# Weight reloads of a recurrent attention layer: keys in rows of 3072 bytes instead of 1536, output weights in three transfers instead of six

## The chip, the cores and the metric

The kernel runs on one core of one Trainium2 chip. The metric is the device time of one execution in microseconds (us), lower is better. Each version is executed several times; one further execution is taken with the hardware profiler and gives the page and the trace that are read below.

## The reference, cut to what matters

Four layers alternate, A, B, A, B. Each is added to a residual stream `x` of 2048 rows and 640 columns in bf16. Layer A is the one that this change touches. It is recurrent: the 2048 rows are cut into 64 segments of 32 rows, each segment is attended together with 8 memory rows, and the memory of a segment is the output of the segment before.

```python
# layer A: 32 heads of 192; M = 8 memory rows, seg_len = 32
mem = mem0
for s in range(n_seg):                                # 64 segments, one after the other
    xs = x[:, s * seg_len:(s + 1) * seg_len, :].copy()
    h = jnp.concatenate([mem, xs], axis=1)            # 40 rows of 640
    q = jnp.einsum('btd,dhe->bhte', h, Wq)            # 640 -> 32 x 192
    k = jnp.einsum('btd,dhe->bhte', h, Wk)
    v = jnp.einsum('btd,dhe->bhte', h, Wv)
    scores = jnp.einsum('bhqe,bhke->bhqk', q, k) * scale
    scores = jnp.where(mask[None, None], scores, -1000000000.0)
    p = _softmax(scores, axis=-1)
    o = jnp.einsum('bhqk,bhke->bhqe', p, v)
    o = jnp.einsum('bhte,hed->btd', o, Wo)            # 32 x 192 -> 640
    mem = o[:, :M, :].copy()                          # feeds the next segment
    outs.append(o[:, M:, :])
```

Layer B is a linear attention over all rows. It is not touched.

## The kernel before, in words

Layer A has two parts. `A_pre` (line 676) computes, for all segments at once, what belongs to the last 8 rows of each segment and doesn't depend on the recurrence. `A_chain` (line 863) then walks the 64 segments in order; it is the recurrent part, and both layers A together walk 128 segments.

The heads are worked on in four rounds (`NR = 4`), each with a quarter of the columns of every weight. A weight piece of one round is named by its matrix (Q, K or V), its round `r` and its block `b` of the 640 inputs (five blocks of 128); it holds 128 partitions of 1536 bf16 values, 3072 bytes a partition. The weights of all four rounds don't fit in the on-chip memory. Most pieces are resident. Of each matrix three pieces live in slots (`SLOTS`, line 18), which hold round 0 or round 3 in turn. So does the output weight of one round, `wo_end`, which is 128 partitions of 7680 values, 15,360 bytes a partition, and holds round 0 or round 3. Its source is `wo_rows`, a copy of the output weights of these rounds that the kernel lays out once in the order of use.

The order of rounds alternates from segment to segment (`rounds`, line 880: 0 1 2 3, then 3 2 1 0), so that a segment starts with the round that the segment before ended with. A segment has to fetch one round: the slots after the first round have been multiplied, and `wo_end` after the first round's output product.

- `project` (line 940) multiplies the segment's 32 new columns with the five pieces of a matrix, four matmuls for each piece. In the first round of a segment (`n == 0`) it takes the slots first and calls `load_slot` (line 618) for each as soon as the four matmuls that read it are in the program. `load_slot` issues one transfer of 3072-byte rows for a Q or V piece, and two of 1536-byte rows for a K piece (line 621). The K product (its view of the weights at lines 952 and 953 takes 32 columns of both halves) needs both halves.
- `wo_round` (line 1039) multiplies one round's attention output with that round's output weights, in six steps of four matmuls (`j` = 0, 2, 4, 6, 8, 10). Step `j` reads the 1280 values from column 640 j of `wo_end` or `wo_mid`, that is one sixth, which is one transfer of `load_wo` (line 635) of 2560-byte rows.
- In the round `n == 2` the program multiplies the first round's output weights (line 1124) and then reloads `wo_end` with `load_wo(order[L])` (line 1125). The last `wo_round` of the segment (line 1173) reads it.

The order of instructions on each engine is written out by hand (`tc.manual_schedule()`, line 870); the framework puts in the waits between engines and transfers. All reloads are issued by SyncE, in the order Q, K, V, `wo_end`. GpSimd issues the small transfers of the chain (`kqb`, `Vp`, `otb`, `xr`, `attn`). After the last `wo_round`, lines 1179 to 1186 turn its result into the memory columns of the next segment's `hT`, for which the next segment's first matmul waits. A few matmuls into a scratch tile (`keep_busy`, lines 1172 and 1175) stand before and after that last product.

Of the kernel before, what the change touches and what calls it, by code (L numbers as in the profile page):

```python
# [115 lines left out]
class Kernel:  # L116
# [468 lines left out]
    def layer_A(self, xn_dram, at_dram, li, x_raw=None):  # L585
        nc, tc = self.nc, self.tc
        KC, NSEG = self.KC, self.NSEG
        dram = self.dram
        NR = 4
        PW = 1536  # L590
        self.kqb_d = dram.tile([NSEG, P, NR, 192], BF16, name=f"kqb{li}")
        self.vb_d = dram.tile([NSEG, NR, 2, 8, 896], BF16, name=f"vb{li}")
        self.otb_d = dram.tile([NSEG, P, 384], BF16, name=f"otb{li}")
        wview = self.wview
        wov = self.A_Wo.rearrange("h d m -> (h d) m").rearrange("(c p) m -> p c m", p=P)
        low = self.view(0, LATE)
        at = LATE
        res, slot = {}, {}
        for r in (3, 2):
            for m in "KQV":  # L600
                for b in range(KC - (SLOTS[m] if r == 3 else 0)):
                    res[m, r, b] = low[:, len(res) * PW:len(res) * PW + PW]
        assert len(res) * PW * 2 == LATE
        for m, r, b in [(m, 0, b) for m in "KQV" for b in range(KC - SLOTS[m])] + \
                [(m, None, b) for m in "KQV" for b in range(KC - SLOTS[m], KC)] + [(m, 1, b) for m in "KQV" for b in range(KC)]:
            v = self.view(at, 2 * PW)
            at += 2 * PW
            if r is None:
                slot[m, b] = v
            else:  # L610
                res[m, r, b] = v
        holds = {}
        wo_mid = self.view(at, 24 * 1280)
        wo_end = self.view(at + 24 * 1280, 12 * 1280)
        assert at + 36 * 1280 == ARENA
        unread = set(res)

        def load_slot(m, r, b, whole=False):
            if holds.get((m, b)) != r:
                holds[m, b] = r  # L620
                w = PW if whole or m in "QV" else PW // 2
                for h in range(0, PW, w):
                    nc.sync.dma_start(out=slot[m, b][:, h:h + w], in_=wview[m][:, b, PW * r + h:PW * r + h + w])

        def load_matrix(m, r):
            for b in range(KC):
                if (m, r, b) in unread:
                    unread.remove((m, r, b))
                    nc.sync.dma_start(out=res[m, r, b], in_=wview[m][:, b, PW * r:PW * r + PW])
                elif (m, r, b) not in res:  # L630
                    load_slot(m, r, b, True)

        early = {(0, 4), (0, 5), (2, 4), (2, 5), (1, 0), (1, 1), (1, 2), (1, 3)}

        def load_wo(r, into=None, part=range(6)):
            t = into if into is not None else wo_end[:, :] if r in (0, 3) else wo_mid[:, 7680 * (r - 1):7680 * r]
            for k in part:
                tk = t[:, 1280 * k:1280 * k + 1280]
                if r in (0, 3):
                    self.last_load = nc.sync.dma_start(out=tk, in_=self.wo_rows[r // 3, :, 1280 * k:1280 * k + 1280])  # L640
                else:
                    c0 = 12 * r + (3 * k if k < 4 else 1 + 6 * (k - 4))
                    step = 2 if k < 4 else 3
                    nc.sync.dma_start(out=tk.rearrange("p (c m) -> p c m", m=640),
                                      in_=wov[:, c0:c0 + step + 1:step, :])

        def piece(m, r, b):
            assert (m, r, b) in res or holds[m, b] == r
            return res[m, r, b] if (m, r, b) in res else slot[m, b]

        if li == 0:
            self.wo_rows = dram.tile([2, P, 7680], BF16, name="wo_rows")

        def lay_out_wo(i):
            rows = self.wo_rows[i].rearrange("p (c m) -> p c m", m=640)
            src = wov[:, 36 * i:36 * i + 12, :].rearrange("p (a t) m -> p a t m", t=3)
            for t, to in ((0, rows[:, 0:8:2, :]), (2, rows[:, 1:8:2, :]), (1, rows[:, 8:12, :])):
                nc.sync.dma_start(out=to, in_=src[:, :, t, :])

        def early_wo():  # L660
            for r in (2, 0, 1):
                load_wo(r, part=[k for k in range(6) if (r, k) in early])

        def late_wo(r, part=range(6)):
            load_wo(r, part=[k for k in part if (r, k) not in early])

        self.A_pre(xn_dram, li, load_matrix, piece, wo_mid, wo_end, lay_out_wo, early_wo, x_raw)
        self.A_chain(xn_dram, at_dram, li, load_slot, piece, load_wo, late_wo, wo_mid, wo_end, low)
        self.post_args = at_dram, wo_mid, wo_end, low

    def two_heads(self, ap):
# [188 lines left out]
        if x_raw is None:  # L860
            self.small.close()

    def A_chain(self, xn_dram, at_dram, li, load_slot, piece, load_wo, late_wo, wo_mid, wo_end, low):
        nc, tc, KC, NSEG = self.nc, self.tc, self.KC, self.NSEG
        scale = float(self.Dh) ** -0.5
        NR = 4
        with tc.tile_pool(name=f"A{li}_ch", reuse_waits="tile", bufs=1) as sp, \
# [12 lines left out]
            def rounds(s):  # L880
                return range(NR) if s % 2 == 0 else range(NR - 1, -1, -1)
# [54 lines left out]
            def place_v():  # L936
                nc.gpsimd.tensor_copy(out=Vs[64:96, :], in_=Vs[96:P, :])  # L937
                fetch_v()
# [64 lines left out]
            def sums(S, E):  # L1003
                one = self.ones_blk[0:96, :]
                nc.tensor.matmul(S[:, 0:320], lhsT=ap3(one, [list(one.ap[0]), [0, P]]), rhs=E[0:96, 0:320], start=True,  # L1005
                                 stop=True, skip_group_check=True)
# [32 lines left out]
            def wo_round(W, r, first, last, OT=OT):  # L1039
                m0 = 16 * (r % 2)  # L1040
                w = wo_end[:, :] if r in (0, 3) else wo_mid[:, 7680 * (r - 1):7680 * r]
                for j in range(0, 12, 2):
                    for g in range(4):
                        i = j + g // 2
                        G, c = (i // 4, i % 4) if i < 8 else (i % 4 // 2, 4 + i % 2)
                        wi = w[:, 640 * i:640 * i + 640].rearrange("p (h e c) -> p e h c", h=2, e=2)
                        nc.tensor.matmul(W[32 * g:32 * g + 32, 0:320], lhsT=OT[:, c, m0 + 32 * G:m0 + 32 * G + 32],  # L1047
                                         rhs=wi[:, g % 2], start=(first and j == 0), stop=(last and j == 10),
                                         tile_position=(0, 32 * g), skip_group_check=True)
# [35 lines left out]
            for s in range(NSEG):  # L1085
                order = rounds(s)
                L = NR - 1

                def q_or_k(m, n):
                    ps = pqp.tile([P, 512], F32, name="ps_qk", tag="qk")  # L1090
                    project(hT, ps, m, n, s)
                    return to_raw(ps, "raw" if n else "OT" if m == "Q" else "rc")
# [28 lines left out]
                for n in range(1, L):  # L1121
                    raw = q_or_k("Q", n + 1)
                    if n == 2:
                        wo_round(W, order[0], True, False)
                        load_wo(order[L])
                        if s == NSEG - 1:
                            load_wo(3, low[:, 0:7680])
                    sums(S, E)
                    O = attend(E)
                    if n == 2:  # L1130
                        place_v()
                    S1 = scores(order[n])
                    rc = reciprocals(S)
                    E = weigh(S1)
                    S = S1
                    to_rows(raw, "Q", order[n + 1])
                    next_kq(s, n)
                    if n == 1 and s + 1 < NSEG:
                        xr = load_rows(s + 1)
                    if n == L - 1:  # L1140
                        to_rows(q_or_k("K", n + 1), "K")
                        scale_out(O, rc)
                    else:
                        rawk = q_or_k("K", n + 1)
                        scale_out(O, rc)
                        to_rows(rawk, "K")
                    store_tail(s, order[n - 1])
                    pv = values(n, pop, "v")
                    v_rows(pv, 0, "s")
                    v_rows(pv, 1, "s")  # L1150
# [27 lines left out]
                if s + 1 < NSEG:  # L1178
                    wt = sp.tile([P, 2, KC, 32], F32, name="wt", tag="rc")
                    wv = W[:, 0:320].rearrange("p (h j b) -> p h b j", h=2, b=KC)  # L1180
                    for b0, b1 in ((2, 5), (0, 2)):
                        nc.vector.transpose(out=wt[:, :, b0:b1, :], in_=wv[:, :, b0:b1, :])  # L1182
                        for h in range(2):
                            a, b = slice(64 * h, 64 * h + 64), slice(64 - 64 * h, 128 - 64 * h)
# [74 lines left out]
```

## Time and profile before

| quantity | value |
|---|---|
| median of 3 runs | 3784.3 us (3781.2 to 3788.56) |
| the profiled execution's own time | 3791.75 us |
| its span, first to last instruction | 3790.0 us |
| granted TensorE clock | 0.98 |
| busy share PE / PEld / DVE / ACT / POOL | 91% / 57% / 58% / 53% / 52% |
| moved by DMA | 933.27 MB, 246 GB/s over the span |
| moved in the two chains of segments (219 to 1610 us and 2132 to 3520 us) | 281 and 280 GB/s, DMA share 0.84 in both |
| one segment (from one first reload of Q, 1001.12 us, to the next, 1022.84 us) | 21.72 us |

PE is the matrix unit, PEld its loading of stationary operands, DVE, ACT and POOL are VectorE, ScalarE and GpSimd, and SPq is SyncE, which here only issues transfers. The page gives, in this order, the busy time of each engine, the span in 40 slices, the DMA queues, the chain of work that ended last, the costliest groups of instructions and the DMA issues. A group's line ends with the idle time of its engine just before it and with what ended that idle time. "DMA share" is the packets' summed time over 16 DMA engines, so a value about 1 says that all 16 worked all the time; it can be a little over 1 because packets of different queues overlap on an engine.

### The profile page before, as it was taken

What the parts mean: (1) busy time and instruction counts of PE and PEld (TensorE: products, weight loads), DVE (VectorE), ACT (ScalarE), POOL (GpSimd) and SP (SyncE); (2) the same over time, 40 slices, a digit from 0 to 9 for tenths busy, and PEclk for the clock granted to TensorE, in tenths of its full rate; (3) what the DMA queues carried; (4) which work ended last, traced back from release to release, by engine and by line L of the source; (5) the groups of instructions that cost most, each with busy time, mean ns of one, the idle gap of its engine ahead of it and who ended that gap; (6) DMA issues with size and microseconds to landing.
All of it is one profiled execution on the core that took longest, in us unless ns stands there. A gap on an engine that the chain in (4) does not pass through costs nothing.

```text
span 3790.0 us, 147033 instructions
## 1 busy us (share of the span) xinstructions
PE 3446.3 (91%) x60058; PEld 2175.8 (57%) x60222; DVE 2180.9 (58%) x5940; ACT 1999.4 (53%) x4517; POOL 1955.7 (52%) x4871
## 2 busy tenths in 40 slices
PE   9979999999999999889899899999999999998898
PEld 6745555555555555555377555555555555555553
DVE  5446656666666666446633566566566665665465
ACT  2345555555555555546423455555555555555463
POOL 3446656666666666430433466566566665664300
PEclk9999999999999999989899999999999999999999
DMA  8988888888888888820477888888888888888300
GB/s 300 308 277 275 290 268 281 288 267 290 283 272 287 274 283 286 294 89 1 143 253 216 276 282 288 267 287 279 268 287 277 278 282 273 272 284 292 104 1 28
DMA packets 531678, 933.27 MB, mean 246 GB/s; under 512 B 145458, under 2 KB 295690, under 8 KB 531002
## 3 DMA queue, kind: packets, MB, share of 16 engines
q1 hardware_dynamic: 428858, 818.87, 63.7%
q0 software_dynamic: 68480, 91.75, 7.9%
q10 hardware_dynamic: 33664, 13.24, 1.4%
q8 instruction: 472, 7.73, 0.9%
q14 instruction: 204, 1.67, 0.1%
HBM read 853.72 MB, written 73.40 MB: 245 GB/s over the span
## 4 chain that ended last, share of the span: by engine, by line
PE 27%; DMA 16%; issue 5%; DVE 4%; ACT 3%; POOL 2%; PEld 2%; SPq 0%; POOLq 0%; DVEq 0%; ACTq 0%
DMA arena<-wo_rows 12%; PE ps_qk L954 9%; PE ps_v L954 3%; DMA arena<-in_A_Wv_dram 2%; PE ps_w L1047 2%; PE ps_qk L391 2%; PE ps_s L994 2%; PE ps_pre L825 1%; PEld L825 1%; DVE wt L1182 1%; PE ps_v L421 1%; DVE hT L1185 1%; PE kv L431 1%; PE ps_o L1019 1%; ACT arena L89 1%
## 5 line engine op out<-in xcount | busy, mean ns | idle before, releaser
L954 PEld LDWEIGHTS <-hT 128*32 128x32 bf16 x30720 | 786.7, 96 | 654.0 <-issue 148.7
L954 PE MATMUL ps_qk<-arena,hT 128*32 128x384 bf16 x20480 | 982.6, 328 | 61.5 <-DVE hT L1185 31.0
L964 ACT ACTIVATE raw<-ps_qk 128x384 bf16<-128x384 f32 x896 | 439.9, 491 | 371.6 <-DVE QT L975 139.8
L954 PE MATMUL ps_v<-arena,hT 128*32 128x384 bf16 x10240 | 515.6, 327 | 79.3 <-DMA arena<-in_A_Wv_dram 74.8
L1047 PE MATMUL ps_w<-arena,OT 128*32 128x320 bf16 x9216 | 428.1, 304 | 83.2 <-DMA arena<-wo_rows 75.7
L981 ACT ACTIVATE Vp<-ps_v 64x384 bf16<-64x384 f32 x896 | 434.0, 484 | 73.2 <-PE ps_v L954 42.6
L973 DVE STREAM_TRANSPOSE QT<-raw 128x256 bf16<-128x256 bf16 x384 | 171.0, 445 | 476.2 <-PE ps_s L994 450.9
L969 DVE STREAM_TRANSPOSE KT<-raw 128x384 bf16<-128x384 bf16 x512 | 296.0, 578 | 174.4 <-ACT raw L964 166.3
L917 POOL DMA_DIRECT2D kqb<-kqb x512 | 288.3, 563 | 177.9 <-POOL KT L926 143.5
L1047 PEld LDWEIGHTS <-OT 128*32 128x32 bf16 x9216 | 231.6, 97 | 249.6 <-issue 111.7
L1037 POOL DMA_DIRECT2D otb<-otb x512 | 280.3, 547 | 167.4 <-POOL otb L1036 143.0
L906 ACT ACTIVATE half<-ps_w 64x160 f32<-64x160 f32 x256 | 76.5, 299 | 514.2 <-PE ps_qk L954 487.2
L1010 ACT ACTIVATE ps_s<-ps_s 128x320 f32<-128x320 f32 x512 | 217.3, 424 | 191.5 <-PE ps_s L1005 190.2
L937 POOL COPY Vp<-Vp 32x896 bf16<-32x896 bf16 x256 | 237.2, 926 | 70.6 <-PE ps_o L1019 52.4
L994 PE MATMUL ps_s<-QT,KT 128*96 128x80 bf16 (+1 forms) x3072 | 245.1, 217 | 24.2 <-POOL KT L926 7.0
L994 PEld LDWEIGHTS <-KT 128*96 128x96 bf16 x3072 | 221.3, 125 | 55.1 <-issue 40.9
L1031 DVE TENSOR_TENSOR OT<-ps_o,rc 64x160 bf16<-64x160 f32 x768 | 243.0, 316 | 9.8
L1019 PE MATMUL ps_o<-E,Vp 96*128 96x80 bf16 x4096 | 233.9, 202 | 1.0 <-ACT ps_s L1010 0.8
L1011 ACT ACTIVATE rc<-ps_s 128x320 f32<-128x320 f32 x512 | 224.1, 438 | 18.4 <-DVE OT L1031 1.6
L1027 DVE TENSOR_TENSOR OT<-ps_o,rc 128x320 bf16<-128x320 f32 x384 | 188.6, 491 | 74.4 <-ACT rc L1011 58.6
L1019 PEld LDWEIGHTS <-Vp 96*128 96x128 bf16 x4096 | 210.0, 100 | 32.0 <-ACT Vp L981 13.6
L1000 ACT ACTIVATE E<-ps_s 96x320 bf16<-96x320 f32 x512 | 218.1, 426 | 12.3 <-PE ps_s L994 9.0
(161 smaller groups left out, 5567.1 us busy)
## 6 DMA issues: line engine op xcount, KB each, us to landing
arena<-wo_rows SPq DMA_DIRECT2D x792, 320.0 KB, 6.7
arena<-in_A_Wq_dram SPq DMA_DIRECT2D x427, 384.0 KB, 4.4
arena<-in_A_Wv_dram SPq DMA_DIRECT2D x427, 384.0 KB, 6.9
arena<-in_A_Wk_dram SPq DMA_DIRECT2D x768, 192.0 KB, 6.3
kqb<-kqb POOLq DMA_DIRECT2D x512, 48.0 KB, 5.3
arena<-in_A_Wk_dram SPq DMA_DIRECT2D x43, 384.0 KB, 6.8
vb<-arena POOLq DMA_DIRECT2D x128, 112.0 KB, 6.0
Vp<-vb POOLq DMA_DIRECT2D x256, 56.0 KB, 5.7
```

Of the source, the lines that this page charges most:

```text
L917: nc.gpsimd.dma_start(out=kqb[:], in_=self.kqb_d[s, :, r, :])
L937: nc.gpsimd.tensor_copy(out=Vs[64:96, :], in_=Vs[96:P, :])
L954: nc.tensor.matmul(ps[32 * g:32 * g + 32, 0:384], lhsT=hT[:, b, :], rhs=rhs, start=(i == 0), stop=(i == KC - 1), tile_position=(0, 32 * g) ...
L964: nc.scalar.activation(out=raw, in_=ps[:, 0:384], func=ACT.Copy)
L969: nc.vector.transpose(out=KT[:, :, 0:64], in_=raw.rearrange("p (c j) -> p c j", j=64))
L981: nc.scalar.activation(out=o, in_=i, func=ACT.Copy)
L994: nc.tensor.matmul(S[0:96, c0:c0 + 80 * (q1 - q0)], lhsT=KT[:, 3 * x + i, :], rhs=QT[:, x, q0:q1, :], start=False, stop=(x == 1 and i == 2 ...
L1011: nc.scalar.activation(out=rc[:, :], in_=S[:, 0:320], func=ACT.Exp, scale=-1.0)
L1019: nc.tensor.matmul(O[:, 80 * c:80 * c + 80], lhsT=Vs[0:96, 448 * x + k:448 * x + k + 128], rhs=E[0:96, 160 * x + 80 * e:160 * x + 80 * e + ...
L1031: nc.vector.tensor_tensor(out=OT[h, 4:6, :], in0=ov[h, 4:6, :], in1=rv[h, :, e, :], op=ALU.mult)
L1037: nc.gpsimd.dma_start(out=self.otb_d[s, :, 96 * r:96 * r + 96], in_=ob[:, :])
L1047: nc.tensor.matmul(W[32 * g:32 * g + 32, 0:320], lhsT=OT[:, c, m0 + 32 * G:m0 + 32 * G + 32], rhs=wi[:, g % 2], start=(first and j == 0), ...
```

## The change

The keys' slots are filled by one transfer of 3072-byte rows each, like those of Q and V. The reload of `wo_end` inside the chain goes by a new function with three transfers of 5120-byte rows, each of which serves two steps of `wo_round`. The bytes, their addresses and the arithmetic stay the same, and so do the loads ahead of the chain (they filled K slots with whole rows already, and use `load_wo`).

```diff
-        def load_slot(m, r, b, whole=False):
+        def load_slot(m, r, b):
             if holds.get((m, b)) != r:
                 holds[m, b] = r
-                w = PW if whole or m in "QV" else PW // 2
-                for h in range(0, PW, w):
-                    nc.sync.dma_start(out=slot[m, b][:, h:h + w], in_=wview[m][:, b, PW * r + h:PW * r + h + w])
+                nc.sync.dma_start(out=slot[m, b], in_=wview[m][:, b, PW * r:PW * r + PW])
...
-                    load_slot(m, r, b, True)
+                    load_slot(m, r, b)
...
+        def reload_wo(r):
+            for c0 in (0, 2560, 5120):
+                nc.sync.dma_start(out=wo_end[:, c0:c0 + 2560], in_=self.wo_rows[r // 3, :, c0:c0 + 2560])
...
                     if n == 2:
                         wo_round(W, order[0], True, False)
-                        load_wo(order[L])
+                        reload_wo(order[L])
                         if s == NSEG - 1:
                             load_wo(3, low[:, 0:7680])
```

The rest of the diff hands `reload_wo` from `layer_A` to `A_chain`.

More of the change, by code (lines that the diff above doesn't have):

```diff
@@ L667, in layer_A @@
         self.A_pre(xn_dram, li, load_matrix, piece, wo_mid, wo_end, lay_out_wo, early_wo, x_raw)
-        self.A_chain(xn_dram, at_dram, li, load_slot, piece, load_wo, late_wo, wo_mid, wo_end, low)
+        self.A_chain(xn_dram, at_dram, li, load_slot, piece, load_wo, reload_wo, late_wo, wo_mid, wo_end, low)
         self.post_args = at_dram, wo_mid, wo_end, low
@@ L861, in A_pre, with A_chain @@
             self.small.close()
-    def A_chain(self, xn_dram, at_dram, li, load_slot, piece, load_wo, late_wo, wo_mid, wo_end, low):
+    def A_chain(self, xn_dram, at_dram, li, load_slot, piece, load_wo, reload_wo, late_wo, wo_mid, wo_end, low):
         nc, tc, KC, NSEG = self.nc, self.tc, self.KC, self.NSEG
```

## The prediction

> **What bounds the kernel now.** I began with the page. PE is busy 91% of the span, yet the chain that ended last gives PE only 27% and one transfer, the reload of `wo_end`, more than any line of PE:
>
> ```profile
> PE 3446.3 (91%) x60058; PEld 2175.8 (57%) x60222; DVE 2180.9 (58%) x5940; ACT 1999.4 (53%) x4517; POOL 1955.7 (52%) x4871
> ...
> PE 27%; DMA 16%; issue 5%; DVE 4%; ACT 3%; POOL 2%; PEld 2%; SPq 0%; POOLq 0%; DVEq 0%; ACTq 0%
> ```
>
> The waits of PE, longest in total first (us in total, times, longest), say where transfers stop it:
>
> ```profile
> PE ps_w L1047 <- DMA arena<-wo_rows: 75.7, 157, 0.9
> PE ps_v L954 <- DMA arena<-in_A_Wv_dram: 74.8, 108, 2.6
> PE ps_qk L954 <- DVE hT L1185: 31.0, 128, 0.4
> ```
>
> Over 128 segments that is 0.59 us a segment for output weights and 0.58 for V, the third row being the recurrence itself. The timeline of one segment (start, duration, instructions, in brackets the idle time before) shows both in place:
>
> ```profile
> 1001.12 1.28 SPq L623 DMA_DIRECT2D arena<-in_A_Wq_dram  x3
> 1002.52 2.92 SPq L623 DMA_DIRECT2D arena<-in_A_Wk_dram  x6
> 1005.66 2.13 SPq L623 DMA_DIRECT2D arena<-in_A_Wv_dram  x3
> 1010.76 2.71 SPq L640 DMA_DIRECT2D arena<-wo_rows  x6
> ...
> 1015.15 0.35 PE L954 MATMUL ps_v<-arena,hT 128*32 128x384 bf16 x4 [0.38 <-DMA arena<-in_A_Wv_dram]
> ...
> 1019.21 0.73 PE L1047 MATMUL ps_w<-arena,OT 128*32 128x320 bf16 x16
> 1020.42 0.32 PE L1047 MATMUL ps_w<-arena,OT 128*32 128x320 bf16 x4 [0.49 <-DMA arena<-wo_rows]
> 1021.24 0.32 PE L1047 MATMUL ps_w<-arena,OT 128*32 128x320 bf16 x4 [0.49 <-DMA arena<-wo_rows]
> ```
>
> Steps j = 8 and j = 10 of the last output product each wait for their own sixth. The memory of the next segment, and so its first reload, hangs on j = 10. That closes the loop: recurrence, release of slots, one queue of reloads, last sixth, recurrence. Is that queue full? Columns of the windows: us, busy PE, PEld, DVE, ACT, POOL, clock, DMA share, GB/s:
>
> ```profile
> 1014.00:1018.00 4.00, 3.62 (x77) 2.46 (x73) 3.38 (x9) 2.91 (x8) 1.74 (x7) 1.00 1.04 372
> 1018.00:1020.00 2.00, 1.92 (x48) 1.06 (x41) 1.24 (x4) 0.54 (x2) 1.64 (x6) 1.00 0.54 191
> 1020.00:1022.00 2.00, 1.08 (x24) 0.58 (x23) 0.38 (x1) 0.00 (x0) 1.07 (x3) 1.00 0.13 34
> ```
>
> Yes, until about 1018; then a few late DMA engines finish alone, and PE waits for the latest. So the time of a segment follows the work of the latest DMA engine on its share of the reloads.
>
> **What the Trainium skill says.** "DMA: Bandwidth & Descriptors", section "Why a DMA increments its semaphore by 16 and not by 1": a transfer counts as landed only when every engine it uses has finished. The windows agree: share 0.54, then 0.13, while PE still waits. Section "Why small descriptors are slow (HBM only)" states a fixed cost of about 3 cycles for each packet and finds joining rows worth it only at 256 bytes or less; the rows below show a cost that 1536-byte rows still feel. Section "SWDGE vs HWDGE vs iDMA" prefers packets of at most 4096 bytes, for GpSimd's transfers; this queue shows no row over 3072 bytes before the change, so 5120 is untested here.
>
> **What a row costs.** I looked for windows in which SyncE's queue carries one kind of row alone (packets, MB, share of 16 engines). K, V and output weights, from the DMA view of 1006.1 to 1009.0, 1010.9 to 1012.5 and 1014.2 to 1017.5:
>
> ```profile
> q1 hardware_dynamic: 684, 0.94, 93.8%
> ```
>
> ```profile
> q1 hardware_dynamic: 200, 0.56, 95.7%
> ```
>
> ```profile
> q1 hardware_dynamic: 517, 1.18, 96.2%
> ```
>
> Share x 16 x window length gives engine time: 43.5, 24.5 and 50.8 us. With two more segments each (K 44.6 us for 0.96 MB and 45.3 for 0.96; V 22.5 for 0.53 and 21.7 for 0.51; output weights 50.2 for 1.12 and 51.3 for 1.12) the sums are 133.4/2.86 = 46.7 ns a kilobyte (1000 bytes) for 1536-byte rows, 68.7/1.60 = 42.9 for 3072 and 152.3/3.42 = 44.5 for 2560. A row of 1536 costs 71.7 ns and one of 3072 costs 131.8, so the line is 11.6 ns a row and 39.1 ns a kilobyte. It gives 43.7 for 2560, near the 44.5 seen, and 41.4 for 5120 (an estimate outside the rows seen).
>
> **The change part by part**, for one segment.
>
> 1. Keys as whole rows: 3 pieces x 393,216 bytes / 16 engines = 73.7 kB an engine; 46.7 - 42.9 = 3.8 ns a kilobyte less: 0.28 us less engine time. The completions saved are in these figures.
> 2. Output weights: 1,966,080 / 16 = 122.9 kB an engine; 43.7 - 41.4 = 2.3 ns less: 0.28 us less. Bounds: nothing, if 5120-byte rows are cut and cost as now; 44.5 - 41.4 = 3.1 ns, that is 0.38 us. I take the line, as it fits three row lengths. Below zero is rival C.
> 3. Together 0.56 us. Packets of two queues overlap (share 1.04 to 1.07), so wall time of an engine falls by 0.56/1.05 = 0.53 us. The late engine has the same number of rows as the others and works back to back, so all of it should arrive at the end.
> 4. Coarser last transfer: j = 8 no longer runs ahead of the last sixth; after the landing come j = 8 and j = 10. A whole product of 24 matmuls takes 1.00 us, four take 0.32, so a step in flow is (1.00 - 0.32)/5 = 0.14 us. Cost 0.14 on the path. At most both lone steps follow each other, 0.32. The wait for the middle third costs nothing while the last third ends later.
> 5. Coarser first reload: its issue waits one step more of the first product, 0.14 us. SyncE has only the two other thirds and the next segment's Q behind it. The backlog of V hides it: V releases PE at 1015.15, over 4 us after the issue at 1010.76. Without that cover, 0.14 us.
> 6. Issues: 12 instead of 18 a segment. Six K issues take 2.92 us; V's follow about 1.4 us sooner. Worth nothing by itself, since the queue has work until then; it also removes SyncE's waits for earlier landings (127.3 us on Q's over the run). GpSimd's small transfers may wait behind a longer packet, some 0.1 us each; they are issued microseconds ahead.
> 7. V's landing moves 0.27 us earlier with part 1 (0.28/1.05), so PE reaches the last product sooner and the last third stays the later of the two.
>
> Sum: -0.53 + 0.14 = -0.39 us a segment. The first segment of each chain has other loads, so 126 segments: -49 us. The profiled execution of 3791.75 us (span 3790.0, 1.75 around it) becomes 3743; the same 49 us off the median of 3784.3 gives 3735.
>
> PE's wait of 1.17 us a segment caps what can be gained: 150 us over all.
>
> **The rivals.**
>
> A, the sum: 3735. For it speaks the back-to-back queue; against it, that 5120 bytes was extrapolated.
>
> B, the longer output rows bring nothing, because they are cut into packets of the old cost: 0.27 - 0.14 = 0.13 us, 16 us in all, 3768. The 4096-byte preference speaks for it, the straight line over three lengths against.
>
> C, slower: the queue moves bytes at a ceiling, so that a row's shorter time turns into waiting elsewhere, and the coarser last third remains: 0.14 x 126 = +18, 3802. It decides as soon as the engine time saved falls below 0.14/0.53 = 26% of the forecast. For it: at share 1.04 the core already moves 372 GB/s. Against it: windows with longer rows moved more (K 362, V 369, output weights 388 GB/s).
>
> D, the late engines are late through other traffic that stretches as the reloads shrink: half of the 0.53 arrives, -0.13 us, 3768 again.
>
> **How the numbers follow.** A 0.58, B 0.20, D 0.09, C 0.13. Case A reaches from the larger row saving without the coarser last step (0.66 x 126 = 83, so 3701) to half its sum (3760). The range goes down to 3700 and up past B and D to 3783, leaving out C and the tails. A measurement of this kernel can't tell under 0.2% (7.6 us) from no change. Faster by more: nearly all of A, most of B and D, 0.80; same 0.07; slower 0.13.
>
> **What would show it.** Right: SyncE's queue with about 110,600 packets fewer (768 transfers of 144, 128 rows and 16 completions each), half of them the keys'; its K windows near 43 ns a kilobyte and output windows near 41; PE's waits on `wo_rows` and V falling by a third or more together; two steps of the last product in flow after one wait; a segment near 21.3 us. Wrong: output windows at 44.5 or two packets to a row (B); equal GB/s with more time a packet (C); a longer tail after 1018 (D). If PE now waits for something that isn't a reload, my reading of the loop was wrong.

## The result, and the profile after

The changed kernel took 3788.13 us, the median of 12 runs (3773.48 to 3796.77), beside 3785.45 us for the kernel before in 12 runs (3775.25 to 3790.82). The ratio is 1.0003, with an interval from 0.9987 to 1.0018: no change that can be told, where 49 us less had been forecast. The profiled execution had a span of 3791.9 us, 3793.59 with what lies around it.

The change did what it says. The page of the changed kernel gives SyncE's queue (packets, MB, share of 16 engines):

```profile
q1 hardware_dynamic: 318266, 818.83, 62.0%
```

Before, the page had 428,858 packets and 63.7% there: 110,592 packets fewer for the same bytes, as worked out. In time of one DMA engine it is 0.637 x 3790.0 = 2414 us before and 0.620 x 3791.9 = 2351 us after, 63 us less, or 0.49 us for each of 128 segments. The forecast had 0.56. So the engines did save nearly what they were to save, and the time did not move. The rows of 5120 bytes stayed whole, so the cutting that rival B rested on didn't happen; in 1015 to 1018.2 us, where they are alone on the queue, the DMA view gives

```profile
q1 hardware_dynamic: 261, 1.18, 96.5%
```

that is 0.965 x 16 x 3.2 us / 1.18 MB = 41.9 ns a kilobyte, beside 43.0 in the window of the prediction before; three such windows together give 42.0, where the line had said 41.4 and the windows before had shown 44.5.

The end of a segment also looks as foretold. The timeline of PE shows one wait and then both last steps in flow, eight matmuls in 0.46 us:

```profile
1019.79 0.73 PE L1049 MATMUL ps_w<-arena,OT 128*32 128x320 bf16 x16
1021.30 0.46 PE L1049 MATMUL ps_w<-arena,OT 128*32 128x320 bf16 x8 [0.78 <-DMA arena<-wo_rows]
1021.57 0.84 PE L1057 MATMUL ps_idle<-arena,ident 128*32 128x384 bf16 x16
```

What PE waits for (us in total, times, longest) holds the surprise:

```profile
PE ps_w L1049 <- DMA arena<-wo_rows: 77.9, 105, 1.3
PE ps_v L956 <- DMA arena<-in_A_Wv_dram: 57.6, 88, 2.8
...
PE ps_v L956 <- issue: 10.9, 22, 1.2
PE ps_w L1049 <- issue: 10.0, 12, 1.9
...
PE ps_qk L956 <- issue: 8.0, 10, 1.4
```

The waits for output weights did not fall and V's fell by 17 us: together 135.5 us after 150.5, where the prediction had named a fall by a third as the sign of being right. And waits put down to "issue" grew, in which nothing that the profile names was missing; "issue waits" below means PE's. With a fourth row of 0.2 us they add up to 29.1 us. Before, the same sum was 6.1:

```profile
PE ps_qk L954 <- issue: 2.4, 5, 0.6
PE ps_v L954 <- issue: 2.2, 6, 0.6
PE ps_w L1047 <- issue: 1.5, 3, 1.1
```

What PE lacks there can be seen around one of them. PE had done 14 of the 24 matmuls of the segment's last product, had stopped in the middle of a step, where no wait for weights begins, and resumed at 608.00 us after 1.90 us:

```profile
608.00 0.58 PE L1049 MATMUL ps_w<-arena,OT 128*32 128x320 bf16 x10 [1.90 <-issue]
```

The DMA queues of 600 to 605.5 us and then of 605.5 to 607 us:

```profile
q1 hardware_dynamic: 381, 1.70, 80.5%
q0 software_dynamic: 130, 0.16, 8.5%
```

```profile
q0 software_dynamic: 37, 0.03, 6.9%
q8 instruction: 1, 0.02, 4.8%
q1 hardware_dynamic: 4, 0.02, 2.7%
```

By the packet records an instruction packet started at 597.57 us, while the reloads filled the queue, and the next one at 605.62 us, when SyncE's queue had nearly run dry; that one ended at 606.78, and PE went on 1.2 us after it. When it was asked for, the trace does not show, so this example doesn't show either that it stood behind the reloads. Nor is all of the 1.90 us its doing: the last third of the output weights landed at 606.65, 0.55 us after PE had stopped.

Such a packet has 16,384 bytes and takes 1.09 us, and there are 472 in either run, beside 120,280 matmuls and weight loads of PE. Each of the 26 issue waits over 0.5 us ended 1.2 to 1.6 us after the end of an instruction packet; for moments taken at random in the chains the median distance is 3.6 us. I conclude that PE had run out of instructions; the profile doesn't name it.

### The profile page after: what moved, and what is told of

It reads as the page before. It is cut to its first block, busy times and chain, and to the rows that moved or that the text cites. A ratio compares the mean times of both kernels' runs of the same rounds, so it can differ in the third digit from the quotient of the medians.

```text
span 3791.9 us, 145879 instructions
## 1 busy us (share of the span) xinstructions
PE 3436.2 (91%) x60058; PEld 2179.4 (57%) x60222; DVE 2181.4 (58%) x5940; ACT 1996.0 (53%) x4517; POOL 1955.4 (52%) x4871
## 4 chain that ended last, share of the span: by engine, by line
PE 44%; DMA 31%; issue 8%; DVE 6%; POOL 4%; ACT 3%; PEld 3%; SPq 0%; POOLq 0%; ACTq 0%; DVEq 0%
DMA arena<-wo_rows 23%; PE ps_qk L956 17%; PE ps_v L956 6%; PE ps_w L1049 5%; PE ps_s L996 3%; DVE wt L1184 2%; PEld L827 2%; DMA otb<-otb 2%; DMA arena<-in_A_Wv_dram 2%; DVE hT L1187 2%; PE ps_o L1021 2%; PE ps_s L1007 2%; PE ps_qk L391 2%; PE ps_s L991 1%; PE ps_pre L827 1%
## 5 line engine op out<-in xcount | busy, mean ns | idle before, releaser
L956 PE MATMUL ps_v<-arena,hT 128*32 128x384 bf16 x10240 | 515.7, 327 | 70.5 <-DMA arena<-in_A_Wv_dram 57.6
L1049 PE MATMUL ps_w<-arena,OT 128*32 128x320 bf16 x9216 | 417.2, 303 | 94.7 <-DMA arena<-wo_rows 77.9
```

The source lines that it names most:

```text
L956: nc.tensor.matmul(ps[32 * g:32 * g + 32, 0:384], lhsT=hT[:, b, :], rhs=rhs, start=(i == 0), stop=(i == KC - 1), tile_position=(0, 32 * g) ...
```

## The experiments

Ratios are to the kernel before, run beside each version on the same chip; 0.001 is 3.8 us. From the packet records I also worked out, over some 120 segments of each kernel, when the last reload packet of a segment ends after its first Q reload, and how long after that step 10 of the last product (`j` = 10) starts:

| kernel | last packet, us (standard error about 0.05) | step 10 after it, median us |
|---|---|---|
| before | 19.61 | 0.53 |
| changed | 19.39 | 0.66 |
| keys alone | 19.49 | 0.53 |
| output weights alone | 19.32 | 0.65 |
| thirds with short rows | 19.51 | 0.66 |

The last column closes the loop as the prediction read it: in most segments step 10 follows the last packet at the same distance, and the coarser last third adds 0.13 us (forecast 0.14). In the second column the changed kernel gains 0.22 us (standard error of a difference about 0.07) where the engines' mean saved 0.49. So less than half of the saving had reached the last packet.

Three theories stood at first. 1: the saved row time reaches the last packet only in part, and the coarse end eats most of that. 2: the forecast's terms are right, and some new wait cancels them. 3: the queue moves bytes at a ceiling (rival C).

### One part at a time

Keys alone (`e1_keys`, edit in the kernel before):

```diff
-                w = PW if whole or m in "QV" else PW // 2
+                w = PW
```

> The kernel before with only the keys changed: one transfer of 3072-byte rows to a K slot, output weights still in six. Theory 1 (the saved row time reaches the last landing only in part, and most of what does is eaten by the coarser last third): in the trace of the changed kernel V lands 0.09 us earlier in the segment, so -0.09 x 126 = -11 us, ratio 0.997, and two separate waits on output weights as before. Theory 2 (the forecast's terms are right, and a new wait that belongs to the whole change cancels them): -0.27 x 126 = -34 us, ratio 0.991. Theory 3 (the queue moves bytes at a ceiling): 0 us.

Measured: 1.0016 (1.0004 to 1.0027), 6 us slower, just clear of no change. SyncE's queue took 63.2% of 3781.2 us, 24 us less engine time, 0.19 us a segment where 0.28 had been forecast. The issue waits added up to 24.4 us. All three theories were off: a part that saves engine time makes the kernel a little slower, and the issue waits come with it.

Output weights alone (`e2_thirds`): `reload_wo` as in the change, `load_slot` as before.

> The kernel before with only the output weights changed: three transfers of 5120-byte rows, keys still in halves. Theory 1: the last landing gains 0.12 us and the coarser last third costs 0.18 to 0.20, so +0.06 to +0.08 us a segment, +8 to +10 us, ratio 1.002 to 1.003. Theory 2: -0.27 + 0.14 = -0.13 us, -16 us, ratio 0.996. Theory 3: +0.14 x 126 = +18 us or more, ratio 1.005.

Measured: 0.9976 (0.9968 to 0.9984), 9 us faster. The queue took 62.8% of 3778.2 us, 41 us less, 0.32 a segment (forecast 0.28). Issue waits 6.2 us, as before. Theory 3 falls, and the sign of theory 1 was wrong; this part comes near the prediction's number (-16 us). The mechanism does so less: 41 us of engine time less 16 for the coarse end would have made 25.

Thirds with rows that stay short (`e4_thirds_short`): gaps of 128 bytes in `wo_rows` keep the two rows of a transfer apart.

```diff
-            self.wo_rows = dram.tile([2, P, 7680], BF16, name="wo_rows")
+            self.wo_rows = dram.tile([2, P, 6 * 1344], BF16, name="wo_rows")
...
+            for c in (0, 2, 4):
+                nc.sync.dma_start(out=wo_end[:, 1280 * c:1280 * c + 2560].rearrange("p (k e) -> p k e", e=1280),
+                                  in_=self.wo_rows[r // 3].rearrange("p (k e) -> p k e", e=1344)[:, c:c + 2, 0:1280])
```

> The kernel before with three transfers for the output weights whose rows stay 2560 bytes (the copy in device memory is laid out with gaps of 128 bytes, so that the rows can't join), keys in halves. It has the coarser last third without the longer rows. Theory 1: +0.18 us a segment less 0.03 for fewer completions, +19 us, ratio 1.005. Theory 2: 0.14 - 0.03, +14 us, ratio 1.004. If the time is that of the kernel before, the coarser last third costs nothing and the cancelling wait is elsewhere.

Measured: 1.0022 (1.0013 to 1.0030), 8 us slower: the coarse end alone, less what fewer completions save. Against `e2_thirds` it prices the longer output rows by themselves: 0.9976 - 1.0022, 17 us, 0.14 us a segment. The engines' mean saved 31 us between these two (63.4% of 3792.3 and 62.8% of 3778.2). So about half of a saving in row time arrives (13 to 22 of 31 us, by the two intervals).

The last third in two transfers again (`e3_last_sixths`, edit in the changed kernel):

```diff
-            for c0 in (0, 2560, 5120):
-                nc.sync.dma_start(out=wo_end[:, c0:c0 + 2560], in_=self.wo_rows[r // 3, :, c0:c0 + 2560])
+            for c0, c1 in ((0, 2560), (2560, 5120), (5120, 6400), (6400, 7680)):
+                nc.sync.dma_start(out=wo_end[:, c0:c1], in_=self.wo_rows[r // 3, :, c0:c1])
```

> The changed kernel with the last third of the output weights in two transfers of 2560-byte rows again, so that step 8 of the last product can run ahead of step 10. Theory 1: the gains stay (0.09 for keys, about 0.10 for output weights) and the cost of the coarse end goes, so -0.19 us a segment, -24 us, ratio 0.994. Theory 2: -0.50 us, -63 us, ratio 0.983, unless the unknown wait is elsewhere, then 0. Theory 3: 0 us.

Measured: 0.9984 (0.9974 to 0.9994), 6 us faster than before and 7 faster than the changed kernel, the latter at the edge of what the two intervals can tell; 24 had been expected. Issue waits 26.1 us: whole keys, and they are there again.

### Is it the row length of keys, or how far SyncE runs ahead?

After these four runs: issue waits of 24 to 29 us with one transfer to a key piece, 6 to 10 with two. Two readings, both guesses so far. R: instruction packets wait longer between longer rows. D (not the prediction's rival D): SyncE runs further ahead, and they wait behind a deeper queue. In the built programs each transfer of SyncE waits on one of eight counters in turn, so on the landing of the eighth before it; in the kernel before this was a visible wait,

```profile
SPq L623 <- DMA arena<-in_A_Wq_dram: 127.3, 179, 2.6
```

which in the changed kernel is down to 9.4 us in 11 waits. With six transfers ahead of V instead of nine, V's first reload goes out at 3.1 us after the first Q reload instead of 5.0.

Whole rows in two transfers of 64 partitions (`e5_keys_by_partitions`):

```diff
-                w = PW if whole or m in "QV" else PW // 2
-                for h in range(0, PW, w):
-                    nc.sync.dma_start(out=slot[m, b][:, h:h + w], in_=wview[m][:, b, PW * r + h:PW * r + h + w])
+                n = P if whole or m in "QV" else P // 2
+                for p in range(0, P, n):
+                    nc.sync.dma_start(out=slot[m, b][p:p + n, :], in_=wview[m][p:p + n, b, PW * r:PW * r + PW])
```

> The kernel before with keys in whole rows of 3072 bytes, but still two transfers to a piece, each for 64 of the 128 partitions: the longer rows without the fewer transfers. In the three kernels with one transfer to a key piece PE's idle time put down to issue was 24 to 29 us over the run, in the three with two transfers 6 to 10, and each such wait over 0.5 us ended 1.2 to 1.6 us after an instruction fetch had landed. Theory D (depth: with fewer transfers SyncE runs further ahead, and PE's instruction fetches come late behind the deeper queue): issue waits back near 6 us, the row saving is left, about 0.10 us a segment: -13 us, ratio 0.9965. Theory R (row length: an instruction packet waits longer between long rows): issue waits 24 us as with whole rows, ratio 1.0016.

Measured: 1.0795 (1.0773 to 1.0817), at a granted clock of 0.964. The issue waits added up to 24.7 us with nine transfers ahead of V, as R had it. I don't count this against D, because the transfers themselves became slow and with them the queue longer in time; that is an argument and not a test. From 1021.5 to 1025.5 us, keys alone on the queue:

```profile
q1 hardware_dynamic: 348, 0.88, 96.1%
```

0.961 x 16 x 4.0 / 0.88 = 69.9 ns a kilobyte for 3072-byte rows, which cost 42.9 in the prediction's windows of V and 46 on average over the kernel before, in transfers over 128 partitions. Why the halves are slower, no run shows. The version with output weights in two thirds and two sixths on top (`e7_partitions_and_last_sixths`) went the same way.

> Both together: key pieces in two transfers of 64 partitions with whole rows, output weights in two thirds and two sixths. Theory D and theory 1: -13 - 18 = -31 us, ratio 0.992. Theory R: 6 - 18 = -12 us, 0.997. Three more issues a segment than the changed kernel's plus one cost nothing, because the queue is full.

Measured: 1.0778 (1.0758 to 1.0798), with issue waits of 27 us.

Whole rows over 128 partitions, and the number of transfers made up with small ones (`e9_keys_and_small`):

```diff
-                w = PW if whole or m in "QV" else PW // 2
+                w = PW
                 for h in range(0, PW, w):
                     nc.sync.dma_start(out=slot[m, b][:, h:h + w], in_=wview[m][:, b, PW * r + h:PW * r + h + w])
+                if m == "K" and not whole:
+                    nc.sync.dma_start(out=self.few[0:16, 2 * b:2 * b + 2], in_=self.wo_rows[0, 0:16, 0:2])
```

> Keys as one transfer of 3072-byte rows to a piece, output weights in six, and after each key transfer one of 4 bytes to 16 partitions (into unused columns), so that SyncE again issues 18 transfers a segment. A transfer waits for the landing of the eighth before it, so V goes out about when it does in the kernel before (5.0 us after the first Q reload), not at 3.1. Keys in whole rows alone gave 1.0016 with 24 us of issue waits on PE. Theory D (SyncE running further ahead delays PE's instruction fetches): issue waits fall to about 6 us, ratio 1.0016 - 18/3785 + at most 0.1 us x 126 for the small transfers, 0.997 to 1.000. Theory R (the 3072-byte rows delay them): issue waits stay near 24 us, ratio 1.0016 or more.

Measured: issue waits 9.2 us instead of 24.4, with the same rows. So R falls, and the waits go as D had it; that the packets stand behind the queue is still inferred. But the time is 1.0033 (1.0020 to 1.0047): taking those 15 us away did not make the kernel faster. V's last reload now goes out at 8.0 us, later than in the kernel before (7.2).

The same in the version of `e3_last_sixths` (`e10_all_and_small`):

> The same small transfers in the kernel with whole keys, two thirds and two sixths of output weights (0.9984 with 26 us of issue waits). Theory D: issue waits near 6 us, ratio 0.9984 - 20/3785 + small transfers, 0.993 to 0.996. Theory R: 0.998 to 1.001.

Measured: issue waits 8.0 us; ratio 1.0000 (0.9988 to 1.0012). Again D in the waits, and nothing in the time.

The kernel before with the small transfers alone (`e11_before_and_small`), twelve transfers ahead of V:

> The kernel before with the three small transfers alone: their own price, and a SyncE that runs less far ahead than before (21 transfers a segment). Theory D: issue waits at or under 6 us; ratio 1.000 to 1.003 (at most 0.1 us a segment for the small transfers). If V, which now goes out later still, leaves DMA engines without work, slower: over 1.003 with a DMA share under 1 between keys and V.

Measured: issue waits 0.7 us, and 1.0420 (1.0398 to 1.0443). V's first reload goes out at 8.1 us, and PE's wait for V rises from 74.8 us to

```profile
PE ps_v L956 <- DMA arena<-in_A_Wv_dram: 177.6, 180, 4.7
```

The expectation's sign is there too: by the packet records SyncE's reloads held the 16 engines for 70% of the time from 8 to 10 us after the first Q reload, and for 96% in the kernel before. Not all of the loss is waiting: the granted clock of this run was 0.965 instead of 0.980 before, and PE was busy for 3493.4 us instead of 3446.3.

So the depth is a balance with two ends. By transfers ahead of V, and the slow ones over 64 partitions apart, the issue waits were 24 to 29 us with six, 27.7 with eight (next run), 6 to 10 with nine, 0.7 with twelve; in the runs with small transfers, issuing V later cost more than it gave. The small transfers' own price can't be taken apart from that of the later V here.

### Does saved engine time reach the end at all?

One half of one key piece is not reloaded (`e8_one_half_key_less`): half of block 3 of the keys keeps the other round's weights, so part of the computation is changed.

```diff
-                for h in range(0, PW, w):
+                for h in range(0, w if m == "K" and b == 3 and not whole else PW, w):
```

> The kernel before without the second half of one key piece's reload in each segment: half of the keys' block 3 keeps the weights of the other round, so part of the computation is changed. It takes 8 rows of 1536 bytes and one completion from each DMA engine, 8 x 73.6 + 9.6 = 0.60 us by the trace of before. Reading of the loop (the segment follows the last packet one to one): -0.60 x 126 = -75 us, ratio 0.980. Rival (only a part of what engines save reaches the end, as the forecast's failure may say): at most half, ratio 0.990 or more.

Measured: 0.9857 (0.9842 to 0.9872), 54 us faster, 0.43 us a segment. The issue waits rose from 6 to 27.7 us here too (eight transfers ahead of V). By the packet records the engines saved 72 us, so three quarters of it arrived, and the rival (at most half) falls.

How much of the issue waits lies on the path can be read from the traces. I took the segments whose last product had an issue wait and added up by how much step 10 came later after the last packet than the kernel's median. Here that is 13.5 us (17 segments, 20.5 us of issue waits), in `e1_keys` 7.8 us (11 segments, 11.2 us) and in the changed kernel 6.4 us (9 segments, 8.7 us). The other issue waits fall mostly into the projections; whether they delay anything is not shown. With the 13.5 us, some 67 of the 72 us are accounted for: bytes left out arrive nearly whole, while row time saved arrived by about half.

### A version that beats both

Keys in halves as before, output weights in two thirds and two sixths (`e6_halves_and_last_sixths`; the edit of `e3_last_sixths` on `e2_thirds`):

> Keys in halves as before; output weights in two transfers of 5120-byte rows and, for the last third, two of 2560-byte rows. The thirds alone gave 0.9976, and step 10 followed the last packet by 0.65 us there and by 0.53 before. Theory 1 as it stands now (output rows save about 0.2 us on the last packet, the coarse end costs 0.12 us): -0.071 - 0.12 + 0.05 for the third that keeps short rows = -0.14 us a segment, -18 us, ratio 0.9953. Rival: the coarse end is not on the path, and the shorter rows of the last third lose again: 0.9985.

Measured: 0.9959 (0.9945 to 0.9973), 16 us faster than before. Issue waits 9.2 us.

One transfer of 10,240-byte rows for the first two thirds (`e12_one_long_and_last_sixths`):

```diff
-            for c0, c1 in ((0, 2560), (2560, 5120), (5120, 6400), (6400, 7680)):
+            for c0, c1 in ((0, 5120), (5120, 6400), (6400, 7680)):
```

> Keys in halves; output weights in one transfer of 10,240-byte rows and two of 2560-byte rows for the last third. Against the version with two thirds and two sixths (0.9959) it joins eight more pairs of rows on each engine and drops one completion: by the line of the prediction 8 x 11.6 + 9.6 = 0.10 us, so 0.9959 - 0.10 x 126/3800 = 0.9926 if the row line holds to 10,240 bytes and all of it arrives. Rival: the first transfer now waits for four steps of the first output product (0.27 us later than with thirds), and DMA engines that are done with V stand idle that long; then 0.996 to 0.998. A second rival: fewer transfers, more issue waits on PE (over 10 us).

Measured: 0.9953 (0.9941 to 0.9964), not to be told from the version with thirds. The packet records give one reason: a row of 10,240 bytes took 439 ns on average, two of 5120 took 443, so joining further saves almost nothing. Issue waits 8.3 us. PE's wait for output weights is the lowest of all versions but the slow `e7_partitions_and_last_sixths` (48.2 us):

```profile
PE ps_w L1051 <- DMA arena<-wo_rows: 49.7, 121, 0.8
```

## Why the prediction was wrong

- **Reading of the bound: right.** The segment follows the last reload packet, and leaving bytes out moves it.
- **Part 1, keys (0.28 us): mis-sized.** Engine time fell by 0.19 us a segment. I took the price of whole key rows from V's windows. But keys follow Q directly, and from 4.0 to 5.5 us of a segment packets take longer than the median of their row length: this excess was 0.17 us an engine before and 0.27 with whole keys (from the packet records). That is about what is missing; why it grows is open.
- **Part 2, output weights (0.28): right**, 0.32 measured.
- **Part 3, "so all of it should arrive at the end": failed, and this is the largest miss.** The prediction let 0.53 us a segment arrive. The engines' mean saved 0.49, and the last packet came 0.22 us earlier. Between `e4_thirds_short` and `e2_thirds`, which differ in the row length and the gaps that keep it short, 17 of 31 us arrived. A hint at the reason lies in the chain of packets that ended last in each segment: two rows of 2560 took 216.2 ns from start to start there and one of 5120 took 212.9, while over all packets the mean durations were 233 and 221. The late engines, which decide, would then save less than the mean that I measured. But the difference of 3 ns comes out between 2 and 9 if the chain is followed back over fewer or more packets, so the reason is open.
- **Part 4, coarse end (0.14): right**, 0.13 measured, and 8 us in `e4_thirds_short` with fewer completions counted in.
- **Part 5: its cover was not tested by itself.**
- **Part 6, "Worth nothing by itself": failed.** With SyncE further ahead of the engines the issue waits rose from 6.1 to 29.1 us. Some 6 us of them can be seen at the last product of the changed kernel; for the rest no delay is shown. So this step failed too, but it is the smaller one as far as the traces tell.
- **Part 7:** V's wait fell, 74.8 to 57.6 us, less than the 34 us that the step implied.
- **Range and sign.** Rival D came nearest: it let half of the 0.53 us arrive. Its reason, other traffic that stretches, was not tested, and it had no part for the new issue waits. B fell with the whole 5120-byte rows, C with `e2_thirds`, which was faster.
- **Two small slips.** The lower end of the range takes 0.66 us of engine time as wall time; by the prediction's own 1.05 it is 0.63, that is 79 us and 3705. And the line of row costs goes through two of the three row lengths by construction, so only the third, missed by 0.8 ns a kilobyte, tested it.

In sum, for 126 segments: the last packet came 0.22 us earlier (-28 us), the coarse end costs 0.13 (+16), late instructions at the last product cost 6. That gives -6 with a standard error of some 9 us, where -5 to +7 was measured. It fits, but it is no close test. What stays open is why so little reaches the last packet, for keys above all: whole keys gained nothing even where the issue waits were gone (`e9_keys_and_small`), and no run removed those waits without touching V's reloads.

## What to carry to other kernels

A shorter time for each row is not yet a shorter time for the engine that finishes last, and only that one counts when a consumer waits for the whole transfer; price it on the late part of the queue, not on its mean. Fewer, larger transfers also let the issuing engine run further ahead. In these runs PE's issue waits rose with that, so look for "issue" waits, see where an instruction packet lands before they end, and ask how much of each wait would have been spent waiting for data anyway. Make the early part of a reload coarse and its last part as fine as the steps that use it: with keys in halves, that took 16 us off (`e6_halves_and_last_sixths`), and thirds throughout took 9 (`e2_thirds`).

## What the runs showed of the hardware that was not expected

- PE stood still for 1.90 us in the middle of a product (at 608 us of the changed kernel) and went on 1.2 us after an instruction packet of 16,384 bytes. Such waits added up to 24 to 29 us with six transfers ahead of V and to 0.7 with twelve.
- Transfers over 64 partitions in rows of 3072 bytes took 69.9 ns a kilobyte, beside 46.7 for 1536-byte rows over 128 partitions, and made the kernel 8% slower.
- Joining rows further than 5120 bytes saved almost nothing: 439 ns for 10,240 bytes against 443 for two rows of 5120.
